# Two of three split score products merged into one 512-column matmul, with two PSUM banks for the scores and two instead of three for the transposes

## The chip, the cores and the metric

One core of one Trainium2 chip runs the program in one launch. The metric is the device time of an execution in microseconds (us), lower is better. The kernel before took 349.04 us as the median of three runs (346.83 to 352.06).

## The reference, cut to what matters

Attention over columns for four batches, whose output feeds a soft mixture of experts. N is 5056 rows, C is 256 columns.

```python
def _attn_ref(q, k, v, tau):                      # (4, 5056, 256) each
    qn = q / (norm(q, axis=1) + 1e-06)
    kn = k / (norm(k, axis=1) + 1e-06)
    s = kn.transpose(0, 2, 1) @ qn / tau          # 256 x 256 per batch, summed over 5056 rows
    a = softmax(s, -1)
    return v @ a

def _moe_ref(x, phi, w1, w2):                     # x: (20224, 256)
    logits = x @ phi                              # 32 slots, 8 experts x 4
    d = softmax(logits, 0)
    slot_out[e] = relu((d.T @ x)[e] @ w1[e]) @ w2[e]
    c = softmax(logits, 1)
    return c @ slot_out
```

## The kernel before, in words

**Tiling.** A batch's 5056 rows come in five chunks of 1024 (the last 960) rows. A chunk of q and k is loaded as two halves, `raw{b}_{ch}_0` and `raw{b}_{ch}_1`, each with four groups `j` of 128 rows; a chunk of v is one tile `v{b}_{ch}`. All loads are issued by SyncE (SP) in program order (L122, L492 to L501): the two halves of a chunk of q and k, then from the eighth chunk on one tile of v behind each. `raw` has five buffers (L129), v has six (VB, L39), and a load waits in SP's queue for its buffer to come free; what stands behind it in the queue waits too.

**Stage A, scores** (`scores_chunk`, L143). Per half, ScalarE rounds the first NS of the four groups to the type fp32r (`hl[:, 0]`, L156), VectorE takes the remainder (`hl[:, 1]`, L157), and ScalarE squares q and k for the norms (L160). TensorE accumulates k^T q over all rows in PSUM tile S, for two halves `m` of k's columns. A split group takes three products with 256 moving columns: high k by high q, high k by low q, low k by high q (L173). An unsplit group takes one product in plain float32, which runs as two matmul instructions. NS is 2 in batch 0 (0 in its first half) and 3 after that. S is one PSUM bank and has one buffer, so batch b+1's first product waits until ScalarE has copied S to `ssb` (L206).

**Attention** (`attention_steps`, L192). The norms go through TensorE (n, nn), then the scale rq, the row maximum, Exp (a), the transpose of a (aTp, L247), and M = a phi (Mp, L254).

**Stage B, soft slots** (`soft_slots`, L469) of batch b runs during stage A of batch b+1, two chunks behind. Each chunk of v is transposed by TensorE in four tiles (vTp, L284) that share the three PSUM buffers of `ps_t` (L64) and are copied out at L291. Then come the logits L (L309), their maximum (peak, rp), the shift (cp, L355), Exp, and `gather_chunk` (G, L397), which multiplies v itself by the weights. G is the last reader of a v tile. Chunks 0 to 2 make the first gather group (G_0) and chunks 3 and 4 the second (G_1).

**Tail and output.** After the last batch's scores, a sequence written out by hand for TensorE (L511 to L692) finishes the last two batches, the experts H and O follow, and then 20 output chunks are computed and stored (L707 to L744).

**What sets the order.** Outside the part by hand, and for SP, a scheduler with its own timeline model decides the order of the instructions on each engine when the program is built, from priorities, buffers and its costs. So an edit in one place can move instructions elsewhere.

Of the kernel before, what the change touches and what calls it, by code (L numbers as in the profile page):

```python
# [8 lines left out]
F32 = mybir.dt.float32  # L9
F32R = mybir.dt.float32r  # L10
AF = mybir.ActivationFunctionType
ALU = mybir.AluOpType
AX = mybir.AxisListType
PSUM = bass.MemoryType.PSUM
# [3 lines left out]
def colnorm_attention_soft_moe(  # L18
# [12 lines left out]
    nc = tc.nc  # L31
    B, N, C = q.shape
    E, _, F = w1.shape
    P = 128
    J = 8
    S = 32
# [16 lines left out]
    while t0 < N:  # L53
        pc = min(P, (N - t0) // J)
# [6 lines left out]
    keep = ctx.enter_context(tc.tile_pool(name="keep", bufs=1))  # L61
    vpool = ctx.enter_context(tc.tile_pool(name="vpool", bufs=VB))
    bpool = ctx.enter_context(tc.tile_pool(name="bpool", bufs=1))
    ps_t = ctx.enter_context(tc.tile_pool(name="ps_t", bufs=3, space=PSUM))  # L64
    ps_b = ctx.enter_context(ExitStack())
    pb = ps_b.enter_context(tc.tile_pool(name="pb", bufs=1, space=PSUM))
    ps_a = ctx.enter_context(ExitStack())
    pa = ps_a.enter_context(tc.tile_pool(name="pa", bufs=1, space=PSUM))
# [54 lines left out]
    st = [dict() for _ in range(B)]  # L123
# [19 lines left out]
    def scores_chunk(b, ch):  # L143
        pc = chunks[ch][1]
        if ch == 0:
            st[b]["S"] = pa.tile([P, 2, C], F32, tag="S", name=f"S{b}")
            st[b]["sum"] = apool.tile([P, G, 2, C], F32, tag="sum", name=f"sum{b}", bufs=1)
        sps, ssum = st[b]["S"], st[b]["sum"]
        sqs = []
        for h in range(2):  # L150
# [12 lines left out]
            for x, j in enumerate(order):  # L163
                first = ch == 0 and h == 0 and x == 0
                last = ch == NCH - 1 and h == 1 and x == HJ - 1
                for m in range(2):
                    cols = slice(P * m, P * m + P)
                    if j >= ns:
                        pairs = [(raw[:pc, 1, j, cols], raw[:pc, 0, j, :])]
                    else:  # L170
                        kh, kl = hl[:pc, 0, 1, j, cols], hl[:pc, 1, 1, j, cols]
                        qh, ql = hl[:pc, 0, 0, j, :], hl[:pc, 1, 0, j, :]
                        pairs = [(kh, qh), (kh, ql), (kl, qh)]  # L173
                    for y, (lhs, rhs) in enumerate(pairs):
                        nc.tensor.matmul(  # L175
                            sps[:, m, :],
                            lhs,
                            rhs,
                            start=first and y == 0 and m == 0,
                            stop=last and y == len(pairs) - 1,  # L180
                            skip_group_check=True,
                        )
        s0, s1 = sqs
# [8 lines left out]
    def attention_steps(b):  # L192
# [4 lines left out]
        for g in range(G):  # L197
# [4 lines left out]
                start=True,  # L202
                stop=True,
            )
        busy = b < B - 1
        nc.scalar.copy(ssb, sps)  # L206
        nc.scalar.copy(nsb, nps)
        yield
        mp = pb.tile([P, 2 * C], F32, tag="amisc", name=f"nn{b}")
# [574 lines left out]
```

## Time and profile before

| | before |
|---|---|
| times of three runs, us | 346.83, 349.04, 352.06 |
| span of the profiled execution, us | 344.0 |
| busy TensorE (PE) / VectorE (DVE) / ScalarE (ACT), us | 304.7 / 250.4 / 237.2 |
| matmuls of the scores, split groups (S<-hl) | 648 instructions, 102.1 us |
| matmuls of the scores, unsplit groups (S<-raw) | 208 instructions, 55.7 us |
| transposes of v (vTp) | 320 instructions, 42.8 us |
| mean granted TensorE clock | 0.972 |

The profile page gives the span from the first to the last instruction of one execution; that execution's own time isn't listed apart, and what lies around the span is about 5 us if it is compared with the median. A row of the timeline view gives start, length, engine, line, operation, tiles and count of a run of equal instructions, and in brackets how long the engine sat idle before it and what ended that. Matmuls are pipelined, so the cost of one is read from start to start and not from its length. PEld is TensorE's weight load, SPq is the queue of SyncE. The stages lie at these times: scores from 7 to 210 us, the tail to about 277 us, the output to 344 us.

### The profile page before, as it was taken

Reading aid. Unit: us, or ns where it says so; the run is one execution under the profiler, and the core shown is the slowest. Engines: PE = TensorE matmul, PEld = TensorE weight load, DVE = VectorE, ACT = ScalarE, POOL = GpSimd, SP = SyncE. Lnnn points to the kernel's source line nnn. Section 1 sums busy time; section 2 is a strip of 40 time slices with the busy share of each in tenths; the row PEclk is TensorE's granted clock in tenths of the full one; section 3 lists DMA queues with packets and bytes.
Section 4 is the critical chain, followed back from the end, with each engine's and each line's share of the span. In section 5 each row is a group of like instructions: output and inputs, shape, how many; then the busy total and the mean of one; then the engine's idle time right before and its main releaser. Section 6 shows DMA issues by size and latency. Waiting matters only on the chain.

```text
span 344.0 us, 6200 instructions
## 1 busy us (share of the span) xinstructions
PE 304.7 (89%) x2460; PEld 238.8 (69%) x2460; DVE 250.4 (73%) x410; ACT 237.2 (69%) x306; POOL 11.4 (3%) x16
## 2 busy tenths in 40 slices
PE   1999969997999999999999899898889998989850
PEld 1888868987788977777896776665644576767530
DVE  1588798995898894988799478478958167986440
ACT  3676769987898995898799396464343348796620
POOL 0000000100000100000100000104000000000000
PEclk9999969999999999899999999999999999999995
DMA  7999989999899429999921994999979408999995
GB/s 248 356 387 243 322 292 326 313 246 356 271 288 340 139 94 265 384 409 266 399 120 29 291 316 104 424 266 412 419 303 418 173 26 342 288 416 356 376 401 209
DMA packets 20244, 100.04 MB, mean 291 GB/s; under 512 B 2744, under 2 KB 2744, under 8 KB 13240
## 3 DMA queue, kind: packets, MB, share of 16 engines
q1 hardware_dynamic: 20216, 99.66, 83.6%
q8 instruction: 19, 0.31, 0.4%
q14 instruction: 9, 0.07, 0.1%
HBM read 78.94 MB, written 20.71 MB: 290 GB/s over the span
## 4 chain that ended last, share of the span: by engine, by line
PE 56%; DMA 15%; DVE 11%; ACT 9%; issue 3%; SPq 2%; POOL 0%; DVEq 0%; ACTq 0%
PE S L175 20%; DMA raw<-in_k_dram 12%; PE vTp L284 7%; PE op L729 5%; PE L L309 4%; PE op L730 4%; DMA v<-in_v_dram 3%; PE G L397 3%; ACT hl L156 3%; ACT sq L160 3%; DVE o L735 2%; PE H L644 2%; PE O L670 2%; PE cTp L718 2%; DVE sq L184 1%
## 5 line engine op out<-in xcount | busy, mean ns | idle before, releaser
L175 PE MATMUL S<-hl 128*128 128x256 f32 (+1 forms) x648 | 102.1, 303 | 2.3 <-DVE hl L157 2.0
L175 PEld LDWEIGHTS S<-hl 128*128 128x128 f32 (+1 forms) x648 | 86.1, 196 | 10.7 <-issue 3.7
L160 ACT ACTIVATE sq<-raw 128x2048 f32<-128x2048 f32 (+1 forms) x40 | 76.8, 1921 | 10.4 <-DMA raw<-in_k_dram 4.7
L157 DVE TENSOR_TENSOR hl<-raw,hl 128x1536 fp32r<-128x1536 f32 (+3 forms) x39 | 63.5, 1628 | 20.8 <-ACT hl L156 20.8
L156 ACT CAST hl<-raw 128x1536 fp32r<-128x1536 f32 (+3 forms) x39 | 53.8, 1379 | 25.4 <-DMA raw<-in_k_dram 13.1
L175 PE MATMUL S<-raw 128*128 128x256 f32 (+1 forms) x208 | 55.7, 401 | 11.7 <-DMA raw<-in_k_dram 9.0
L184 DVE TENSOR_TENSOR sq<-sq,sq 128x2048 f32<-128x2048 f32 (+1 forms) x20 | 45.8, 2288 | 6.9 <-ACT sq L160 6.6
L175 PEld LDWEIGHTS S<-raw 128*128 128x128 f32 (+1 forms) x208 | 38.9, 202 | 16.5 <-issue 9.4
L284 PE MATMUL vTp<-ident,v 128*128 128x128 f32 (+1 forms) x320 | 42.8, 275 | 3.1 <-DMA v<-in_v_dram 2.8
L291 ACT COPY vT<-vTp 128x512 f32<-128x512 f32 (+1 forms) x70 | 39.1, 588 | 8.8 <-PE vTp L284 7.8
L284 PEld LDWEIGHTS vTp<-ident,v 128*128 128x128 f32 (+1 forms) x320 | 35.4, 142 | 9.8 <-issue 6.0
L729 PE MATMUL op<-soh,cT 128*128 128x512 f32 (+1 forms) x80 | 34.1, 426 | 4.5 <-ACT o L733 2.3
L733 ACT COPY o<-op 128x1024 f32<-128x1024 f32 (+1 forms) x26 | 26.3, 1023 | 10.1 <-PE op L730 10.1
L730 PE MATMUL op<-sol,cT 128*128 128x512 f32 (+1 forms) x80 | 31.6, 395 | 0.0
L735 DVE COPY o<-op 128x1024 f32<-128x1024 f32 (+1 forms) x14 | 17.1, 1224 | 13.0 <-PE op L730 13.0
L309 PE MATMUL L<-vT,M 128*32 128x256 f32 (+1 forms) x320 | 22.8, 383 | 1.7 <-DVE cm L566 1.5
L185 DVE TENSOR_TENSOR sq<-sq 128x1024 f32<-128x1024 f32 (+1 forms) x20 | 24.3, 1213 | 0.0
L729 PEld LDWEIGHTS op<-soh,cT 128*128 128x128 f32 (+1 forms) x80 | 14.9, 186 | 12.7 <-DVE o L735 5.7
L397 PE MATMUL G<-v,dn 128*32 128x256 f32 (+1 forms) x320 | 20.0, 382 | 0.5 <-DVE zacc L385 0.5
L723 ACT CAST cT<-cTp 128x512 fp32r<-128x512 f32 (+1 forms) x20 | 11.7, 588 | 10.3 <-PE cTp L718 5.3
L730 PEld LDWEIGHTS op<-sol,cT 128*128 128x128 f32 (+1 forms) x80 | 15.0, 187 | 2.4
L397 PEld LDWEIGHTS G<-v,dn 128*32 128x32 f32 (+1 forms) x320 | 9.8, 109 | 7.0 <-ACT gs L426 1.0
(122 smaller groups left out, 284.6 us busy)
## 6 DMA issues: line engine op xcount, KB each, us to landing
raw<-in_q_dram SPq DMA_DIRECT2D x32, 512.0 KB, 8.2
raw<-in_k_dram SPq DMA_DIRECT2D x32, 512.0 KB, 8.9
v<-in_v_dram SPq DMA_DIRECT2D x16, 1024.0 KB, 9.2
w<-in_moe_w_dram SPq DMA_DIRECT2D x16, 1024.0 KB, 16.5
out_dram<-o SPq DMA_DIRECT2D x15, 1024.0 KB, 6.7
raw<-in_q_dram SPq DMA_DIRECT2D x8, 480.0 KB, 9.6
raw<-in_k_dram SPq DMA_DIRECT2D x8, 480.0 KB, 11.3
v<-in_v_dram SPq DMA_DIRECT2D x4, 960.0 KB, 16.6
```

The costliest lines, as they stand in the source:

```text
L156: nc.scalar.copy(hl[:pc, 0, :, :ns], raw[:pc, :, :ns])
L157: nc.vector.tensor_tensor(hl[:pc, 1, :, :ns], raw[:pc, :, :ns], hl[:pc, 0, :, :ns].bitcast(F32), op=ALU.subtract)
L160: nc.scalar.activation(sq[:pc], raw[:pc], AF.Square)
L175: nc.tensor.matmul(sps[:, m, :], lhs, rhs, start=first and y == 0 and m == 0, stop=last and y == len(pairs) - 1, skip_group_check=True,)
L184: nc.vector.tensor_tensor(s0[:pc], s0[:pc], s1[:pc], op=ALU.add)
L284: nc.tensor.transpose(tp[:, jj, :pc], vt[:pc, 4 * hh + jj, P * m : P * m + P], ident[:pc, :pc])
L291: nc.scalar.copy(dst, tp[:, :, :pc])
L309: nc.tensor.matmul(L[S * g : S * g + S, :, :w], M[:, m, :], st[b]["vT", ch, m][:, :, S * g : S * g + w], start=m == 0, stop=m == 1,)
L397: nc.tensor.matmul(gp[S * g : S * g + S, :], dn[ch - lo][:pc, j, :], vt[:pc, j, :], start=ch == lo and j < G, stop=ch == hi - 1 and j >= G,)
L729: nc.tensor.matmul(dst, cT[:, 2 * hh + jj, :pc], soh, start=True, stop=False)
L730: nc.tensor.matmul(dst, cT[:, 2 * hh + jj, :pc], sol, start=False, stop=True)
L733: nc.scalar.copy(od, op[:pc])
```

## The change

For a split group, high k by high q and high k by low q have the same weights. They become one matmul with 512 moving columns, whose result has two halves: S grows to [128, 2, 2, 256], two PSUM banks, one for each `m`. Low k by high q (256 columns) is added to the second half. The first half holds the high products and the unsplit groups. At the end of a batch ScalarE copies the first half to `ssb`, and VectorE adds the second half to it. To make room, `ps_t` gets two buffers instead of three.

```diff
-    ps_t = ctx.enter_context(tc.tile_pool(name="ps_t", bufs=3, space=PSUM))
+    ps_t = ctx.enter_context(tc.tile_pool(name="ps_t", bufs=2, space=PSUM))
...
-            st[b]["S"] = pa.tile([P, 2, C], F32, tag="S", name=f"S{b}")
+            st[b]["S"] = pa.tile([P, 2, 2, C], F32, tag="S", name=f"S{b}")
...
                     if j >= ns:
-                        pairs = [(raw[:pc, 1, j, cols], raw[:pc, 0, j, :])]
+                        todo = [(sps[:, m, 0], raw[:pc, 1, j, cols], raw[:pc, 0, j, :])]
                     else:
                         kh, kl = hl[:pc, 0, 1, j, cols], hl[:pc, 1, 1, j, cols]
-                        qh, ql = hl[:pc, 0, 0, j, :], hl[:pc, 1, 0, j, :]
-                        pairs = [(kh, qh), (kh, ql), (kl, qh)]
-                    for y, (lhs, rhs) in enumerate(pairs):
+                        todo = [(sps[:, m], kh, hl[:pc, :, 0, j, :]), (sps[:, m, 1], kl, hl[:pc, 0, 0, j, :])]
+                    for y, (dst, lhs, rhs) in enumerate(todo):
                         nc.tensor.matmul(
-                            sps[:, m, :],
+                            dst,
                             lhs,
                             rhs,
-                            start=first and y == 0 and m == 0,
-                            stop=last and y == len(pairs) - 1,
+                            start=first and y == 0,
+                            stop=last and y == len(todo) - 1,
                             skip_group_check=True,
                         )
...
-        nc.scalar.copy(ssb, sps)
+        nc.scalar.copy(ssb, sps[:, :, 0])
+        nc.vector.tensor_tensor(ssb, ssb, sps[:, :, 1], op=ALU.add)
         nc.scalar.copy(nsb, nps)
```

In the changed kernel the lines from the products on stand one higher (the matmul is L174, ScalarE's copy L205), up to the added line, which is L206; behind it the numbers are as before.

The scheduler's order changes with it, above all on TensorE. First place: TensorE in stage A of batch 2, around the gather G_0 of batch 0, which frees the first three v tiles. Before:

```order
118 L175 MATMUL S_1021<-raw_3_0_214 128x256 x2
119 L397 MATMUL G_0_994<-v_0_172,dn_0_991 32x256 x8
120 L397 MATMUL G_0_994<-v_1_180,dn_0_991 32x256 x8
121 L397 MATMUL G_0_994<-v_2_188,dn_0_991 32x256 x8
122 L284 MATMUL vTp_0_1_1_1329<-ident,v_0_212 128x128 x4
123 L175 MATMUL S_1021<-hl_3_0_1350 128x256 x18
124 L175 MATMUL S_1021<-raw_3_1_217 128x256 x2
...
129 L175 MATMUL S_1021<-hl_3_1_1375 128x256 x13
130 L284 MATMUL vTp_1_0_0_1403<-ident,v_1_220 128x128 x4
...
133 L175 MATMUL S_1021<-raw_4_0_222 128x256 x2
```

The same place in the changed kernel, from the last product of hl_3_1 on:

```order
359 L174 MATMUL S_927<-hl_3_1_1239 128x256
...
368 L397 MATMUL G_0_900<-v_0_172,dn_0_897 32x256 x8
369 L397 MATMUL G_0_900<-v_1_180,dn_0_897 32x256 x8
370 L397 MATMUL G_0_900<-v_2_188,dn_0_897 32x256 x4
371 L254 MATMUL Mp_838<-phi_sb,aT_836 128x32 x4
372 L338 MATMUL rp_1_1092<-ident,mx_1_1090 1x128
...
376 L284 MATMUL vTp_1_0_0_1261<-ident,v_1_220 128x128 x4
377 L309 MATMUL L_0_1207<-vT_0_0_1179,M_843 32x256 x4
...
382 L174 MATMUL S_927<-raw_4_0_222 128x256 x2
383 L284 MATMUL vTp_1_1_1_1280<-ident,v_1_220 128x128 x4
384 L309 MATMUL L_1_1286<-vT_1_0_1260,M_843 32x256 x4
385 L174 MATMUL S_927<-hl_4_0_1299 128x512
```

G_0 has moved behind all products of hl_3_0, raw_3_1 and hl_3_1, so that no score product is left between it and raw_4_0; between them now stand the rest of G_0, Mp, rp, five transposed tiles, L_0 and cp.

Second place: TensorE in stage A of batch 3, around G_0 of batch 1. Before:

```order
202 L175 MATMUL S_1630<-hl_3_0_1962 128x256 x4
203 L397 MATMUL G_0_1603<-v_0_212,dn_0_1597 32x256 x8
204 L397 MATMUL G_0_1603<-v_1_220,dn_0_1597 32x256 x8
205 L397 MATMUL G_0_1603<-v_2_228,dn_0_1597 32x256 x8
...
210 L175 MATMUL S_1630<-hl_3_0_1962 128x256 x11
211 L175 MATMUL S_1630<-raw_3_1_258 128x256 x2
212 L175 MATMUL S_1630<-hl_3_1_1987 128x256 x13
213 L338 MATMUL rp_1_1819<-ident,mx_1_1817 1x128
214 L254 MATMUL Mp_1538<-phi_sb,aT_1536 128x32 x4
...
219 L175 MATMUL S_1630<-raw_4_0_263 128x256 x2
220 L175 MATMUL S_1630<-hl_4_0_2053 128x256
```

The same place in the changed kernel:

```order
534 L174 MATMUL S_1477<-hl_3_0_1773 128x256
535 L174 MATMUL S_1477<-raw_3_1_258 128x256 x2
536 L397 MATMUL G_0_1450<-v_0_212,dn_0_1444 32x256 x8
537 L397 MATMUL G_0_1450<-v_1_220,dn_0_1444 32x256 x4
538 L254 MATMUL Mp_1385<-phi_sb,aT_1383 128x32 x4
...
545 L309 MATMUL L_0_1760<-vT_0_0_1732,M_1390 32x256 x4
...
557 L174 MATMUL S_1477<-hl_3_1_1792 128x256
...
562 L174 MATMUL S_1477<-raw_4_0_263 128x256 x2
563 L174 MATMUL S_1477<-hl_4_0_1852 128x512
```

G_0 has moved behind hl_3_0 and raw_3_1; of the products of that chunk only hl_3_1 is left between it and raw_4_0, and the whole of hl_4_0 follows raw_4_0 at once, where one product, L_0 and a tile of vTp stood before.

Third place: VectorE at the end of batch 0, where S is handed over. Before:

```order
29 L187 TENSOR_TENSOR sum_274<-sq_3_0_399 128x512
30 L157 TENSOR_TENSOR hl_0_0_545<-raw_0_0_154,hl_0_0_545 128x1536
31 L184 TENSOR_TENSOR sq_4_0_444<-sq_4_0_444,sq_4_1_465 120x2048
32 L157 TENSOR_TENSOR hl_0_1_570<-raw_0_1_157,hl_0_1_570 128x1536
33 L185 TENSOR_TENSOR sq_4_0_444<-sq_4_0_444 120x2x512
```

In the changed kernel:

```order
29 L186 TENSOR_TENSOR sum_274<-sq_3_0_379 128x512
30 L157 TENSOR_TENSOR hl_0_0_510<-raw_0_0_154,hl_0_0_510 128x1536
31 L183 TENSOR_TENSOR sq_4_0_416<-sq_4_0_416,sq_4_1_433 120x2048
32 L206 TENSOR_TENSOR ssb_454<-ssb_454,S_273 128x512
33 L157 TENSOR_TENSOR hl_0_1_529<-raw_0_1_157,hl_0_1_529 128x1536
```

The new add that releases S stands behind the long addition of the squares sq_4_0. SP's order of loads is the same in both.

## The prediction

> **What bounds the kernel now.** I read the page first, for the share of each engine, then the waits of SP's queue, then TensorE's timeline at the two places where those waits are longest.
>
> ```profile
> PE 304.7 (89%) x2460; PEld 238.8 (69%) x2460; DVE 250.4 (73%) x410; ACT 237.2 (69%) x306; POOL 11.4 (3%) x16
> L175 PE MATMUL S<-hl 128*128 128x256 f32 (+1 forms) x648 | 102.1, 303 | 2.3 <-DVE hl L157 2.0
> L175 PEld LDWEIGHTS S<-hl 128*128 128x128 f32 (+1 forms) x648 | 86.1, 196 | 10.7 <-issue 3.7
> ```
>
> TensorE is busy 89% of a span of 344.0 us, and the products that change are its largest group: 648, so 216 triples. That makes the change look as if it worked on the bound. But a length isn't a cost here, and the second view shows what TensorE is kept waiting for.
>
> ```profile
> SPq L140 <- PE G L397: 34.3, 3, 19.1
> ```
>
> SP stands with a load of v at its head until a gather frees a buffer, 34.3 us in three waits of up to 19.1, and the loads of q and k stand behind it. The two places on SP, and the first on TensorE:
>
> ```profile
> 112.56 0.44 SPq L132 DMA_DIRECT2D raw<-in_k_dram  x1
> 125.35 0.33 SPq L140 DMA_DIRECT2D v<-in_v_dram  x1
> 126.21 0.40 SPq L132 DMA_DIRECT2D raw<-in_k_dram  x1
> 187.02 0.33 SPq L140 DMA_DIRECT2D v<-in_v_dram  x1
> ```
> ```profile
> 124.22 2.80 PE L397 MATMUL G<-v,dn 128*32 128x256 f32 x48
> 126.95 0.66 PE L284 MATMUL vTp<-ident,v 128*128 128x128 f32 x4
> 127.36 2.40 PE L175 MATMUL S<-hl 128*128 128x256 f32 x18
> 129.59 1.03 PE L175 MATMUL S<-raw 128*128 128x256 f32 x4
> 130.27 0.95 PE L175 MATMUL S<-hl 128*128 128x256 f32 x5
> ...
> 135.73 1.10 PE L175 MATMUL S<-raw 120*128 120x256 f32 x4 [0.76 <-DMA raw<-in_k_dram]
> 136.76 0.38 PE L355 MATMUL cp<-negone,rowrun 1*128 1x1 f32 x2
> 137.07 1.08 PE L254 MATMUL Mp<-phi_sb,aT 128*128 128x32 f32 x8
> 137.98 0.36 PE L175 MATMUL S<-hl 120*128 120x256 f32 x1
> 138.99 3.05 PE L175 MATMUL S<-hl 120*128 120x256 f32 x17 [0.64 <-DVE hl L157]
> ```
>
> The reader is to see a race. The first v tile's share of G_0 ends at 124.22 + 2.73/3 = 125.13 us, and 0.2 us later SP issues v and then raw_4_0. That data is usable 10.6 us after the gather (135.73) in raw form and 13.9 us after it (138.99) split. TensorE fills nearly all of this with score products that were loaded earlier, and idles 0.76 + 0.64 = 1.4 us. The same at the second place:
>
> ```profile
> 185.89 2.80 PE L397 MATMUL G<-v,dn 128*32 128x256 f32 x48
> 197.94 1.10 PE L175 MATMUL S<-raw 120*128 120x256 f32 x4 [1.23 <-DMA raw<-in_k_dram]
> 199.43 0.39 PE L175 MATMUL S<-hl 120*128 120x256 f32 x1 [0.39 <-ACT hl L156]
> 201.47 2.29 PE L175 MATMUL S<-hl 120*128 120x256 f32 x17
> ```
>
> So in stage A the time is set by TensorE's work in order plus whatever of this latency it can't fill. Both depend on where the scheduler puts G_0.
>
> **The merged product.** From the chain of waits, the pitch of the 256-column products; from the output stage's timeline, the 512-column products of this type, with a weight load each (the first and the last of four rows in a row).
>
> ```profile
> 80.73 2.05 PE S L175 x17
> ```
> ```profile
> 321.69 0.39 PE L730 MATMUL op<-sol,cT 128*128 128x512 f32 x1
> ...
> 322.38 0.39 PE L729 MATMUL op<-soh,cT 128*128 128x512 f32 x1
> ```
>
> 2.05/17 is 0.121 us; 322.38 - 321.69 is three steps of 0.230 us. A triple goes from 3 x 0.121 = 0.362 to 0.230 + 0.121 = 0.351 us: 11 ns less, times 216 = **2.4 us less**. The streamed columns are the same, and the weight loads already run beside the products (17 of both in 2.05 us). Bounds: the merged product as dear as two gives 0; as cheap as one 256-column product it gives 216 x 0.121 = 26 us. I take 2.4, since the row with the same width is in the trace.
>
> The Trainium skill, "TensorE: Matmul & The Clock Gate", section "Part 3", says that a weight load overlaps matmuls in flight only when the row group differs. By that 216 loads would come off the path; the pitch above speaks against it, and its price stands under the rivals.
>
> **G_0 moved, batch 2.** In the new order (shown above) all score products that can run without the new load stand ahead of G_0. What is left behind G_0's first tile, ahead of raw_4_0, with steps from start to start:
>
> ```profile
> 118.30 1.36 PE L284 MATMUL vTp<-ident,v 128*128 128x128 f32 x11
> 119.41 0.36 PE L175 MATMUL S<-hl 128*128 128x256 f32 x1
> 119.71 1.06 PE L309 MATMUL L<-vT,M 128*32 128x256 f32 x16
> 120.70 2.18 PE L175 MATMUL S<-hl 128*128 128x256 f32 x16
> ```
>
> The rest of G_0, 2 x 0.91; Mp, 137.98 - 137.07 = 0.91; cp, 137.07 - 136.76 = 0.31, and rp priced like it; five tiles of vTp at 4 x 1.11/11 = 0.40, 2.0; L_0, 0.99. Sum 6.3 us. The data comes after 10.6, so TensorE waits 4.3. Then raw_4_0 (130.27 - 129.59 = 0.68), a tile of vTp (0.40) and half of L_1 (0.5) bring it to 12.2, and the first split product, which now reads high and low q at once, waits to 13.9: 1.7 more. Together 6.0 against 1.4: **4.6 us more**. The work that moved ahead isn't lost, it is done in a time that was full anyway; lost is the cover. SP's queue restarts later by the same move, and the transfers keep their length. Bounds: 0, if G_0 comes early enough that TensorE idles ahead of it anyway, to 13.9 - 1.4 = 12.5, if nothing covers it.
>
> **G_0 moved, batch 3.** First tile done at 185.89 + 0.91 = 186.80. Data after 11.1 us (197.94). The split is ready after ScalarE and VectorE, at 197.90 + 1.48 + 1.77 = 201.15, so 14.4 us after the gather:
>
> ```profile
> 137.18 1.77 DVE hl L157
> 197.90 1.48 ACT hl L156
> ```
>
> Left as cover: the rest of G_0 1.8, Mp 0.9, rp and cp 0.6, four tiles of vTp 1.6, L_0 1.0, hl_3_1 6 x 0.351 = 2.1: 8.0 us. Wait 3.1, then raw 0.68, and hl_4_0 waits 14.4 - 11.8 = 2.6. Together 5.7 against 1.23 + 0.39 = 1.6: **4.1 us more**, with bounds as before.
>
> **The clock behind a stall.**
>
> ```profile
> 40.00:50.00 10.00, 7.08 (x34) 6.11 (x33) 9.66 (x8) 8.91 (x7) 0.00 (x0) 0.73 0.91 325
> 140.00:150.00 10.00, 10.00 (x91) 7.75 (x91) 8.39 (x14) 9.19 (x12) 0.00 (x0) 0.83 1.02 413
> 190.00:200.00 10.00, 8.38 (x64) 7.02 (x64) 3.85 (x7) 4.31 (x5) 0.00 (x0) 1.00 1.02 272
> ```
>
> In these windows PEclk (third number from the right) is 0.73 and 0.83 behind idle stretches of TensorE, and 1.00 at the second stall, which was short. 0.83 of 10 us is 3.4 us at half clock, 1.7 us of work. A longer second stall should cost that too: **1.7 us more** (0 to 3.4).
>
> **S is released later.** The end of batch 0:
>
> ```profile
> 45.09 0.56 ACT L206 COPY ssb<-S 128x512 f32<-128x512 f32 x1
> 45.21 2.29 DVE L184 TENSOR_TENSOR sq<-sq,sq 120x2048 f32<-120x2048 f32 x1
> 45.70 2.07 PE L175 MATMUL S<-raw 128*128 128x256 f32 x4 [2.74 <-ACT ssb L206]
> ```
> ```profile
> L187 DVE TENSOR_TENSOR sum<-sq 128x512 f32<-128x512 f32 x16 | 10.8, 678 | 0.1
> ```
>
> The new add stands behind sq_4_0 in VectorE's order, so it starts at 47.5, takes about 0.68 (as the equally wide L187) and lets TensorE on at 48.2 instead of 45.7. That is 2.5 us, of which the clock was half in these windows, so at most 1.3 us of work; as DMA is 0.91 busy there, I count half: **0.7 us** (0 to 2.5). At the end of batch 1 only L_0 (1.0 us) stands between the last product and the next S, against a copy and an add of 0.56 + 0.68 with their handshakes: **0.6 us** (0 to 2). At the end of batch 2 two tiles of vTp, half of L_2 and gtp stand there and cover it.
>
> **Two buffers for the transposes.** In the stalls the waits for them are covered; in the tail, where 8 tiles follow each other at a few places, **0.5 us** (0 to 2). In the output stage the transposes only lose one chunk of lead, 0.
>
> Sum: -2.4 + 4.6 + 4.1 + 1.7 + 0.7 + 0.6 + 0.5 = +9.8 us on a span of 344.0. The span lies 5 us under the median of the runs; what lies around it doesn't change. Forecast 349.0 + 9.8 = **358.8 us**, 2.8% slower.
>
> **The rivals.** First, *the race is relocated but not lost* (not slower): G_0 late in order, but the score products ahead of it find their data late, so that TensorE idles ahead of G_0 and the latency overlaps that idle time. For it: VectorE and ScalarE are near full at 100 to 125 us. Against it: the rows of TensorE shown from 118 to 135 us have no idle time. Then the two stalls and the clock cost nothing net: 349.0 - 2.4 + 1.8 = 348.4 us. It decides from the point where TensorE idles 4 us or more ahead of each G_0.
> Second, *the removed loads were on the path* (faster): 216 x 86.1/648 = 28.7 us less at most; with the stalls still there 349.0 + 9.8 + 2.4 - 28.7 = 332.5 us. Against it stands the pitch of 0.121 us. This is the price from rows of the overlap rule named above, and I give it 0.03.
> Third, *everything adds up*: half clock behind both stalls and the hand-overs at their upper bounds, 358.8 + 1.7 + 1.8 + 1.4 + 1.5 = 365.2 us.
>
> **How the numbers follow.** Forecast 0.54, first rival 0.30, second 0.03, third 0.13. The forecast's own spread is about 4 us; 2% (7 us, about what a measurement of this kernel tells from no change) lies at 356.0. Slower: 0.42 of the forecast and the third, 0.55. Same: 0.12 of the forecast and 0.26 of the first rival, 0.38. Faster: 0.04 of the first rival, which can win when the new order is luckier, and the second, 0.07. The range reaches from the first rival's time to the third's: 348.0 to 365.5 us, with some 0.2 outside.
>
> **What would show it.** Right: products of S with 512 columns at a step of 0.23 us; the row of raw products behind G_0 in batches 2 and 3 with an idle time of 3 to 5 us released by the DMA, and the split ones behind with 1 to 3 us released by VectorE; the first row of S in batch 1 waiting for VectorE's ssb, near 48 us. Wrong: idle rows ahead of G_0, or stalls of under 2 us with TensorE's work ending as early as before; a step near 0.12 us for 512 columns would overturn the first term.

## The result, and the profile after

The changed kernel takes **362.77 us** as the median of four runs (361.09 to 364.42); the kernel before took 348.23 on the same occasion. The ratio is 1.040 with a 95% interval of 1.032 to 1.048: 4% slower, some 14.5 us, where the forecast was 9.8 us. Ratios are taken over undisturbed runs alone and medians over all, so the two can differ a little, and the profiles of e3, e9 and e12 below are of disturbed runs. The profiled execution took 364.42 us with a span of 362.5.

First the page and the waits of SP's queue, in the changed kernel:

```profile
PE 308.0 (85%) x2244; PEld 227.4 (63%) x2244; DVE 253.9 (70%) x414; ACT 237.6 (66%) x306; POOL 14.6 (4%) x16
L174 PE MATMUL S<-hl 128*128 128x256 f32 (+3 forms) x432 | 94.2, 366 | 4.3 <-DVE hl L157 4.1
```
```profile
SPq L140 <- PE G L397: 41.0, 3, 21.1
```

216 matmuls are gone and TensorE is busy 3.3 us longer all the same. Its share fell from 89% to 85% because the span grew by 18.5 us. SP waits 41.0 us for gathers instead of 34.3. Then SP's timeline, and TensorE's at the two places that the prediction speaks of:

```profile
114.97 0.43 SPq L132 DMA_DIRECT2D raw<-in_k_dram  x1
136.56 0.33 SPq L140 DMA_DIRECT2D v<-in_v_dram  x1
...
138.72 0.40 SPq L132 DMA_DIRECT2D raw<-in_k_dram  x1
```
```profile
135.43 2.37 PE L397 MATMUL G<-v,dn 128*32 128x256 f32 x40
...
142.63 0.63 PE L284 MATMUL vTp<-ident,v 128*128 128x128 f32 x4 [2.05 <-DMA v<-in_v_dram]
143.19 1.49 PE L309 MATMUL L<-vT,M 128*32 128x256 f32 x16
144.61 1.97 PE L284 MATMUL vTp<-ident,v 128*128 128x128 f32 x8
...
147.02 1.16 PE L174 MATMUL S<-raw 120*128 120x256 f32 x4
...
150.19 2.04 PE L174 MATMUL S<-hl 120*128 120x512 f32 x10 [1.01 <-DVE hl L157]
...
196.19 1.50 PE L397 MATMUL G<-v,dn 128*32 128x256 f32 x24
...
207.54 1.10 PE L174 MATMUL S<-raw 120*128 120x256 f32 x4 [1.41 <-DMA raw<-in_k_dram]
210.82 2.72 PE L174 MATMUL S<-hl 120*128 120x512 f32 x7 [2.18 <-DVE hl L157]
```

The order is as predicted: G_0 of batch 2's stretch starts at 135.43 (124.22 before), the next load goes out behind it at 136.56, and raw_4_0 runs at 147.02, 11.3 us later than before. The idle time shows in brackets: 2.05 + 1.01 = 3.1 us, and 1.41 + 2.18 = 3.6 us at the second place. Third, the starts of batches 1, 2 and 3 and the wait between the first two; the row behind them is the wait for v in batch 1 of the kernel before:

```profile
46.90 1.65 PE L174 MATMUL S<-raw 128*128 128x256 f32 x3 [4.72 <-DVE ssb L206]
70.98 1.06 PE L284 MATMUL vTp<-ident,v 128*128 128x128 f32 x8 [4.30 <-DMA v<-in_v_dram]
96.47 1.13 PE L174 MATMUL S<-raw 128*128 128x256 f32 x4 [1.91 <-DVE ssb L206]
...
161.94 1.13 PE L174 MATMUL S<-raw 128*128 128x256 f32 x4 [1.05 <-DVE ssb L206]
```
```profile
80.10 0.63 PE L284 MATMUL vTp<-ident,v 128*128 128x128 f32 x4 [2.16 <-DMA v<-in_v_dram]
```

Batch 1 starts 1.2 us later than before (45.70), batch 2 3.7 us later (its first raw product stood at 92.80 before). All three batches now wait for the new add on VectorE; the kernel before waits 2.74 us at the start of batch 1 and has no idle time at the starts of batches 2 and 3. Fourth, stretches of 10 us with the granted clock, the third number from the right:

```profile
40.00:50.00 10.00, 5.28 (x20) 4.21 (x19) 8.95 (x8) 7.20 (x6) 0.00 (x0) 0.74 0.84 308
70.00:80.00 10.00, 9.02 (x47) 7.99 (x48) 4.36 (x6) 4.95 (x6) 0.00 (x0) 0.83 0.81 223
140.00:150.00 10.00, 7.13 (x52) 4.62 (x50) 5.86 (x13) 5.75 (x9) 0.00 (x0) 0.83 1.01 265
210.00:220.00 10.00, 9.18 (x68) 7.01 (x69) 7.37 (x12) 7.16 (x12) 0.00 (x0) 0.73 0.96 284
```

Read in windows of 0.8 us, and as long as TensorE has products left, the clock is at half in stretches of 3.4 us or two of them in a row: before, near 44 and 140 us (10.2 us in all, so 5.1 us lost); after, near 44, 72, 143, 208 and, in the experts' stage, 273 us (23.9 us, 11.9 lost).

**Where the 18.5 us of the two spans lie.** The spans differ by more than the medians do. In every run on record the time is 1.7 to 1.9 us above the span, not the 5 us that a comparison with the median of other executions gave, so the profiled execution of the kernel before took some 345.8 us, less than any of its four timed ones, and that of the changed kernel is its slowest.

Up to the product that ends the experts' stage (fo, 277.6 us before and 291.7 after) it is 14.1 us. Of these, 3.7 come before batch 2 starts and 8.2 from there to the last score product. In that stretch TensorE's idle time, added up from its timeline, grew from 3.0 to 7.7 us (+4.7): 3.6 at the two places behind G_0 and 1.05 at the hand-over of S to batch 3. The time lost at half clock grew from 1.7 to 5.1 us (+3.4), but 1.1 of that falls on the idle time ahead of 210.82 and is counted already, which leaves 2.3. Behind the scores it is 2.2, of which one more stretch at half clock is 1.7. So 3.7 + 4.7 + 2.3 + 1.7 = 12.4 us are placed and 1.7 are not. The other 4.4 us lie behind fo, where the engines do the same work in the same time and only the last transfers land later; whether this part belongs to the change is open, and the last section comes back to it.

### The profile page after: what moved, and what is told of

It is laid out like the page before. It is cut to its first block, busy times and chain, and to the rows that moved or that the text cites. A ratio compares the mean times of both kernels' runs of the same rounds, so it can differ in the third digit from the quotient of the medians.

```text
span 362.5 us, 5767 instructions
## 1 busy us (share of the span) xinstructions
PE 308.0 (85%) x2244; PEld 227.4 (63%) x2244; DVE 253.9 (70%) x414; ACT 237.6 (66%) x306; POOL 14.6 (4%) x16
## 4 chain that ended last, share of the span: by engine, by line
PE 49%; DMA 14%; DVE 14%; ACT 11%; issue 5%; SPq 2%; POOL 1%; DVEq 0%; ACTq 0%; POOLq 0%
PE S L174 18%; DMA raw<-in_k_dram 11%; PE vTp L284 7%; PE op L729 5%; ACT sq L160 5%; PE op L730 4%; DMA v<-in_v_dram 3%; DVE hl L157 3%; PE L L309 3%; PE H L644 2%; PE G L397 2%; PE cTp L718 2%; PE O L670 2%; DVE o L735 2%; DVE sq L184 2%
## 5 line engine op out<-in xcount | busy, mean ns | idle before, releaser
L174 PE MATMUL S<-hl 128*128 128x256 f32 (+3 forms) x432 | 94.2, 366 | 4.3 <-DVE hl L157 4.1
L174 PEld LDWEIGHTS S<-hl 128*128 128x128 f32 (+1 forms) x432 | 71.0, 199 | 20.5 <-DVE hl L157 6.3
L157 DVE TENSOR_TENSOR hl<-raw,hl 128x1536 fp32r<-128x1536 f32 (+3 forms) x39 | 63.5, 1628 | 14.4 <-ACT hl L156 14.1
L174 PE MATMUL S<-raw 128*128 128x256 f32 (+1 forms) x208 | 54.9, 398 | 16.2 <-DMA raw<-in_k_dram 8.5
L174 PEld LDWEIGHTS S<-raw 128*128 128x128 f32 (+1 forms) x208 | 38.5, 200 | 22.7 <-DVE ssb L206 8.6
L284 PE MATMUL vTp<-ident,v 128*128 128x128 f32 (+1 forms) x320 | 45.0, 280 | 8.1 <-DMA v<-in_v_dram 7.0
L284 PEld LDWEIGHTS vTp<-ident,v 128*128 128x128 f32 (+1 forms) x320 | 36.0, 144 | 18.4 <-issue 14.4
L291 ACT COPY vT<-vTp 128x512 f32<-128x512 f32 (+1 forms) x70 | 38.2, 583 | 12.5 <-PE vTp L284 12.4
L309 PE MATMUL L<-vT,M 128*32 128x256 f32 (+1 forms) x320 | 24.4, 390 | 1.5 <-DVE cm L566 1.5
L735 DVE COPY o<-op 128x1024 f32<-128x1024 f32 (+1 forms) x14 | 17.1, 1225 | 11.9 <-PE op L730 11.9
L729 PEld LDWEIGHTS op<-soh,cT 128*128 128x128 f32 (+1 forms) x80 | 14.9, 186 | 11.9 <-ACT o L733 4.9
L214 POOL TENSOR_TENSOR rn<-rn,half 128x4 f32<-128x4 f32 x4 | 7.9, 1970 | 166.9 <-DVE rn L213 116.5
## 6 DMA issues: line engine op xcount, KB each, us to landing
w<-in_moe_w_dram SPq DMA_DIRECT2D x16, 1024.0 KB, 15.1
```

What stands on the lines that cost most here:

```text
L157: nc.vector.tensor_tensor(hl[:pc, 1, :, :ns], raw[:pc, :, :ns], hl[:pc, 0, :, :ns].bitcast(F32), op=ALU.subtract)
L174: nc.tensor.matmul(dst, lhs, rhs, start=first and y == 0, stop=last and y == len(todo) - 1, skip_group_check=True,)
L284: nc.tensor.transpose(tp[:, jj, :pc], vt[:pc, 4 * hh + jj, P * m : P * m + P], ident[:pc, :pc])
L291: nc.scalar.copy(dst, tp[:, :, :pc])
L309: nc.tensor.matmul(L[S * g : S * g + S, :, :w], M[:, m, :], st[b]["vT", ch, m][:, :, S * g : S * g + w], start=m == 0, stop=m == 1,)
L729: nc.tensor.matmul(dst, cT[:, 2 * hh + jj, :pc], soh, start=True, stop=False)
```

## The experiments

The theory was the prediction's: the order that came with the merged product puts G_0 late, the next load of q and k queues behind it, and TensorE runs dry. The rivals: the merged product itself, the two banks with their add, or something else in the new order. All the runs beside each other first; "idle" and "lost" are TensorE's idle time, and the time lost to half clock, from the first product of batch 2 to the last of batch 3 in the profiled execution; half clock that falls on idle time is in both. The ratio is to the kernel before, timed on the same chip.

| kernel | median us | ratio, 95% interval | batch 2 starts | batch 3 ends | idle | lost |
|---|---|---|---|---|---|---|
| before | 348.2 | 1 | 92.8 | 209.7 | 3.0 | 1.7 |
| changed | 362.77 | 1.040 [1.032, 1.048] | 96.5 | 221.6 | 7.7 | 5.1 |
| e1 changed, scores behind G_0 | 363.24 | 1.040 [1.031, 1.048] | 93.1 | 217.9 | 8.8 | 3.4 |
| e2 before, G_0 late | 359.53 | 1.031 [1.022, 1.040] | 94.8 | 223.0 | 8.3 | 1.7 |
| e3 unmerged | 349.60 | 0.997 [0.992, 1.003] | 97.4 | 208.2 | 0.0 | 0 |
| e10 unmerged, again | 350.51 | 1.010 [1.007, 1.014] | 94.7 | 206.1 | 0.5 | 0 |
| e4 merged, order of e3 | 350.25 | 1.006 [1.000, 1.013] | 95.4 | 205.4 | 0.0 | 0 |
| e11 the same, again | 354.93 | 1.018 [1.011, 1.025] | 98.4 | 212.6 | 1.5 | 3.1 |
| e5 unmerged, changed order | 363.14 | 1.035 [1.023, 1.046] | 95.7 | 221.0 | 6.8 | 5.1 |
| e6 changed, 7 v buffers | 358.98 | 1.029 [1.021, 1.037] | 98.2 | 215.8 | 3.5 | 3.4 |
| e7 before, 7 v buffers | 344.36 | 0.989 [0.983, 0.995] | 93.0 | 206.5 | 0.0 | 0 |
| e8 changed order, 7 v buffers | 354.15 | 1.022 [1.018, 1.027] | 96.8 | 213.9 | 3.2 | 0 |
| e9 order of e3, 7 v buffers | 351.45 | 0.999 [0.992, 1.006] | 100.5 | 211.7 | 0.0 | 1.7 |
| e12 as e8, add earlier | 351.80 | 1.018 [1.010, 1.026] | 96.8 | 213.9 | 3.2 | 0 |

**e1: undo the place of G_0 in the changed kernel.** The split products of chunk 3 in batches 2 and 3 are queued behind G_0.

```diff
+                        g0 = st[b - 2].get("G0") if b >= 2 and ch == 3 and j < ns else None
+                        with tc.issue_after(g0) if g0 is not None else nullcontext():
-                        nc.tensor.matmul(
+                            nc.tensor.matmul(
...
-            nc.tensor.matmul(
+            t = nc.tensor.matmul(
...
+        if gi == 0 and ch == hi - 1:
+            st[b]["G0"] = t.ins
```

> The changed kernel, complete, with one constraint on the order: the split products of chunk 3 of batches 2 and 3 stand behind the gather G_0 of the batch before last, as they roughly did before the change. Theory (the new order places G_0 late, SP's queue restarts late, and the latency of its loads lies bare): the idle time of TensorE at raw_4_0 and hl_4_0 falls from 3.1 and 3.6 us to under 2 us each, and the time falls by 7 to 11 us from 362.8 to 352 to 356 us. Rival A (the later release of S and the two transpose buffers cost by themselves, wherever G_0 stands): 360 us or more. Rival B (the merged product is itself dearer): 360 us or more.

Measured: 363.24 us, nothing won, so by its time e1 fits the two rivals and not the theory. TensorE's timeline of this kernel, where line 176 is the score product and 399 the gather:

```profile
126.78 0.66 PE L286 MATMUL vTp<-ident,v 128*128 128x128 f32 x4 [1.67 <-ACT vT L293]
...
129.87 2.37 PE L399 MATMUL G<-v,dn 128*32 128x256 f32 x40 [0.41 <-DVE sm L242]
...
142.38 1.03 PE L176 MATMUL S<-raw 120*128 120x256 f32 x4
145.25 1.07 PE L176 MATMUL S<-hl 120*128 120x512 f32 x4 [1.85 <-DVE hl L157]
```

and VectorE's row for the weights `dn` that G_0 multiplies by, in this kernel, in the changed one and in the one before:

```profile
128.86 0.95 DVE L370 STREAM_TRANSPOSE dn<-lt 128x768 f32<-128x768 f32 x1
```
```profile
132.28 0.95 DVE L368 STREAM_TRANSPOSE dn<-lt 128x768 f32<-128x768 f32 x1
```
```profile
119.52 0.97 DVE L368 STREAM_TRANSPOSE dn<-lt 128x768 f32<-128x768 f32 x1
```

The reader is to see that G_0 starts as soon as `dn` is done (128.86 + 0.95 = 129.81), with TensorE idle ahead of it; the bracket names the short instruction behind `dn` on the same engine. It couldn't have come earlier. Not G_0 alone but the whole chain that feeds it, from the logits through the maximum and the shift, stands later in the new order: `dn` by 12.8 us in the changed kernel and by 9.3 us here. Even in the changed kernel `dn` is done only 2.2 us before G_0 starts (132.28 + 0.95 against 135.43). The score products that were held back lost as cover what they gave as lead: idle 8.8 us instead of 7.7. The waits at raw_4_0 and hl_4_0 did shrink, to 1.85 us and, at the second place, 2.18; the others grew. So the theory needed an amendment: the order decides, but G_0's place is the last link of it, and moving that link by itself buys nothing.

**e2: the reverse, a late G_0 in the kernel before.** The gathers of batches 0 and 1 are queued behind the chunk-3 products of batches 2 and 3.

```diff
-                        nc.tensor.matmul(
+                        st[b]["mm"] = nc.tensor.matmul(
...
-                gather(b, gi)
+                (late.append((b, gi)) if b < 2 else gather(b, gi))
...
+            if ch == NCH - 2 and b >= 2:
+                with tc.issue_after(st[b]["mm"].ins):
+                    for ch2 in range(*groups[b - 2][0]):
+                        gather_chunk(b - 2, 0, ch2)
+                finish(b - 2, 0)
+                gather(b - 2, 1)
```

> The kernel before, complete, with nothing of the change in it but the place of the gathers: those of batches 0 and 1 stand behind the last split product of chunk 3 of batches 2 and 3. Theory: TensorE idles 3 to 6 us at each of the two places, waiting for raw_4_0 and hl_4_0, and the time rises by 7 to 11 us to 355 to 360 us. Rivals A and B: it stays within 3 us of the kernel before, at 346 to 351 us.

Measured: 359.53 us, in the theory's range. Three of TensorE's rows with idle time behind the two late gathers:

```profile
139.86 2.82 PE L284 MATMUL vTp<-ident,v 128*128 128x128 f32 x12 [2.06 <-DMA v<-in_v_dram]
...
147.69 1.57 PE L175 MATMUL S<-hl 120*128 120x256 f32 x11 [0.36 <-DVE hl L157]
...
211.34 1.10 PE L175 MATMUL S<-raw 120*128 120x256 f32 x4 [1.09 <-DMA raw<-in_k_dram]
```

Late gathers make the old kernel 3% slower, with the same releasers as in the changed kernel. Behind the first gather TensorE idles 2.4 us, less than the 3 to 6 expected, and behind the second 3.2. The scheduler also moved other work of TensorE along with the gathers, so e2 isn't as clean as the square below. Idle time and half clock grew by 5.3 us together and batch 2 started 2.0 us later; the rest of some 10 us isn't placed.

**e3: one part alone.** The changed kernel with its two banks, add and two vT buffers, but with three products of 256 columns.

```diff
-                        todo = [(sps[:, m], kh, hl[:pc, :, 0, j, :]), (sps[:, m, 1], kl, hl[:pc, 0, 0, j, :])]
+                        qh, ql = hl[:pc, 0, 0, j, :], hl[:pc, 1, 0, j, :]
+                        todo = [(sps[:, m, 0], kh, qh), (sps[:, m, 1], kh, ql), (sps[:, m, 1], kl, qh)]
```

> The changed kernel with the merged product taken apart again: three products of 256 columns into the two banks; the two banks, the add on VectorE and the two transpose buffers stay. The scheduler then places G_0 ahead of the products of hl_3_0 in batch 2 and ahead of raw_3_0 in batch 3, so early or earlier than before the change. Theory: no stall over 2 us at raw_4_0, and 350 to 355 us, what the hand-overs and buffers cost and no more. Rival A: 358 us or more, since all that it blames is still there. Rival B: about 348 us.

Measured: 349.60 us, level with the kernel before (350.51 and 1% above it when repeated, as e10). That lies between the theory's 350 to 355 and rival B's 348. The banks, the add and the buffers aren't the loss, or at most 1% of it. But this edit also gives another order, so it doesn't yet tell the merged product from the order.

**e4 and e5: the square.** To part the two, the order itself is written down. A table in the kernel names, for TensorE, ScalarE and VectorE, the place of every instruction, and an edge without a wait ties each to the one ahead of it. SP's order is the program's in all these kernels. e4 has merged products in the order of e3; e5 has three products in the order of the changed kernel.

```diff
+    pin(tc, nc)
+
+PIN = {
+    "PE": [
+        "0-115 133-153 116-119 154-163 120-123 217-224 164-177 225-232 178-191 124 269-276 192-205 277-284",
...
+def pin(tc, nc):
...
+        for x, y in zip(place, place[1:]):
+            tc.add_manual_dep(
+                mine[y],
+                mine[x].name,
+                mybir.DependencyInfo(mybir.DependencyClass.NoSync, mybir.DependencyReason.DATA),
+                reason="order",
+            )
```

> The changed kernel, its merged products kept, but the instructions of TensorE, ScalarE and VectorE are forced into the order that the kernel with three 256-column products (previous experiment, 349.6 us) has. Theory (the loss sits in the order that came with the merged product, not in the product): 346 to 350 us, G_0 of batch 2 near 125 us, and the merged product worth 0 to 2.4 us beside 349.6. Rival (the merged product itself costs, since its first product waits for high and low q of the whole half): 355 us or more.

> The other corner of the same square: three 256-column products, two banks, the add, but TensorE, ScalarE and VectorE forced into the order of the changed kernel (each merged product replaced by its two at the same place). Theory (order alone): 361 to 367 us, as the changed kernel or up to 2.4 us above it, with raw_4_0 of batch 2 near 147 us. Rival (the merged product itself): 349 to 353 us.

Measured: e4 350.25 us, e5 363.14 us. Whichever product is used, the changed kernel's order costs some 13 us by the medians (363.14 - 350.51 with e10 below, 362.77 - 350.25; with e11 below in e4's place it is 7.8). These kernels ran on several chips; by the ratios to the kernel before on the same chip it is 2.2 to 3.4%, some 8 to 12 us. Whichever order is used, the merged product changes nothing that these times show. TensorE's timeline of e4 at the first place, and its SP wait:

```profile
122.95 2.35 PE L397 MATMUL G<-v,dn 128*32 128x256 f32 x34
...
139.39 0.60 PE L174 MATMUL S<-raw 120*128 120x256 f32 x2
...
140.58 1.62 PE L174 MATMUL S<-hl 120*128 120x512 f32 x7
```
```profile
SPq L140 <- PE G L397: 38.1, 3, 17.2
```

G_0 is at 122.95, and no row up to raw_4_0 and the split products behind it has a bracket. SP still waits 38.1 us, more than in the kernel before (34.3), and TensorE doesn't idle for it here, for it has other work. In e5 the brackets are back, at or close to the places where the changed kernel has them:

```profile
145.62 1.88 PE L175 MATMUL S<-raw 120*128 120x256 f32 x4 [1.45 <-DMA raw<-in_k_dram]
...
207.69 2.04 PE L175 MATMUL S<-raw 120*128 120x256 f32 x4 [2.54 <-DMA raw<-in_k_dram]
210.97 1.44 PE L175 MATMUL S<-hl 120*128 120x256 f32 x5 [1.02 <-DVE hl L157]
```

The difference closes within 1 us. From batch 2's start to batch 3's end the changed kernel takes 125.1 us and e4, with the same products, 110.0: 15.1 more. Of that 7.7 is idle time and 5.1 half clock, with 1.1 counted in both. The remaining 3.4 is in the main work that the changed kernel does here and e4 behind the scores, where e4 takes 2.6 us longer (54.0 against 51.4 us from the last score product to the first of the experts).

**e6 and e7: take away what makes the load wait.** A seventh buffer for v, in the changed kernel and, as a control, in the one before. The room comes from the first expert's weights, which are now loaded with the others.

```diff
-    VB = 6
+    VB = 7
...
-    w1t[0] = keep.tile([P, 2, F], F32, name="w1_0")
...
-        if i == WI:
-            nc.sync.dma_start(w1t[0], w1[0].rearrange("(p d) f -> p d f", d=2))
...
-        for e in range(max(1, G * r), G * r + G):
+        for e in range(G * r, G * r + G):
```

> The changed kernel with seven buffers for v instead of six (the room comes from w1 of the first expert, which is loaded with the other weights, later). The load of raw_4_0 no longer queues behind a load of v that waits for G_0. Theory of the prediction (the stalls behind G_0 are the loss): idle time of TensorE at raw_4_0 and hl_4_0 of batches 2 and 3 falls from 6.7 us to under 2, the half clock behind it goes too, 353 to 357 us. Rival (the whole work of the earlier batch runs late, and G_0 is only its last visible part): 360 us or more.

> The kernel before with the same seventh buffer, as a control. Its stalls behind G_0 were 3.0 us together, so at most that is to be had: 345 to 350 us by either theory. If it is over 352 us, the later load of the first expert's weights has a price of its own, which then has to be taken off the run with seven buffers in the changed kernel.

Measured: 358.98 and 344.36 us. Both gained some 4 us, so the distance stayed, which fits neither expectation for e6 well. Its trace says why. The scheduler gave a new order again, with raw_4_0 ahead of G_0, so the stall at raw_4_0 is gone, and another idle stretch came up further on:

```profile
137.77 0.62 PE L397 MATMUL G<-v,dn 128*32 128x256 f32 x2
...
155.93 1.08 PE L309 MATMUL L<-vT,M 128*32 128x256 f32 x8 [3.53 <-DVE nat L327]
```

As an experiment on the buffer e6 is spoiled: it moves two things. In the kernel before, where the order changed as well, the seventh buffer leaves no idle time in batches 2 and 3 (3.0 us without it) and no half clock there; e7 is the fastest kernel of this study, 1.1% below the kernel before (0.5 to 1.7%).

**e8: the seventh buffer, with the changed kernel's order held fast** by the same kind of table.

> The changed kernel with seven buffers for v, but this time TensorE, ScalarE and VectorE are forced into exactly the order of the changed kernel, so that the buffer is the only difference (in the run before the scheduler had also given another order). Theory of the prediction (the load of raw_4_0 waits for G_0 through the v buffer): TensorE's idle time at raw_4_0 and hl_4_0 of batches 2 and 3 falls to under 2 us, the batches take 4 to 8 us less together, 354 to 358 us. Rival (the whole work of the earlier batch stands late in the order, and another load waits instead): 360 us or more.

Measured: 354.15 us, inside the theory's range. The four places in its timeline, and its SP wait:

```profile
144.05 1.13 PE L174 MATMUL S<-raw 120*128 120x256 f32 x4
...
147.21 2.38 PE L174 MATMUL S<-hl 120*128 120x512 f32 x12 [1.03 <-DVE hl L157]
...
203.09 1.13 PE L174 MATMUL S<-raw 120*128 120x256 f32 x4
...
205.12 2.27 PE L174 MATMUL S<-hl 120*128 120x512 f32 x11 [0.90 <-DVE hl L157]
```
```profile
SPq L140 <- PE G L397: 28.2, 3, 14.8
```

Of the 6.7 us at these places 1.9 are left, both waits for a transfer are gone, and so is the half clock in batches 2 and 3. From batch 2's start to batch 3's end it takes 117.1 us instead of 125.1. The idle time fell by 4.5 and the half clock by 5.1; that is more than the 8.0 us, since 1.1 us of the half clock fell on idle time and is counted in both. By the medians it is 8.6 us, by the ratios 1.8% or some 6. So the load that waits for the gather, in this order, is 6 to 8.6 of the 14.5 us lost, about half, unless part of the gain comes with a seventh buffer in any order, which e9 leaves open. For the other half no experiment names a single cause.

**e9: the buffer in the good order.** The table of e4 with seven buffers.

> Merged products, seven buffers for v, and the order of the kernel with three 256-column products. With six buffers this order left TensorE no idle time in batches 2 and 3, so by the theory (a buffer helps only where a load waits behind a late gather) the seventh gains under 1.5 us: 348 to 351 us beside about 350. Rival (the buffer is worth its 4 us in any order, as it was in the kernel before and in the changed one): 344 to 347 us, level with the kernel before with seven buffers (344.4).

Measured: a median of 351.45 us over twelve runs from 343.45 to 354.68, with a ratio of 0.999 [0.992, 1.006] beside e4's 1.006 [1.000, 1.013]. The intervals overlap: the times exclude neither the theory's gain of under 1.5 us nor the rival's 4. The traces agree with the theory, as neither kernel has idle time in batches 2 and 3 for the buffer to take away.

**e10 and e11: e3 and e4 again, side by side, to size the product.**

> Three 256-column products with two banks, the add and two vT buffers again, as the partner of the next run on the same chip. By the first measurement 348 to 351 us, within 1% of the kernel before.

> Merged products in the order of the run before, on the same chip, to size the product by itself: the order of every engine is the same, so the difference of the two medians is the price of the merge. The prediction's term: 2.4 us less than the run before. Rival (a first product that waits for high and low part of q, or the same pitch per column, eats it): within 1 us of it or above.

Measured: 350.51 and 354.93 us; the ratios are 1.010 [1.007, 1.014] and 1.018 [1.011, 1.025]. The merged product isn't 2.4 us faster; whether it is slower is open, since the same kernel gave 1.006 in e4. In the trace its gain is there and small. One half of a chunk has six triples. In the prediction's rows of the kernel before, 18 products of hl start at 127.36 and the raw products behind them at 129.59: 2.23 us. In the changed kernel, 12 products:

```profile
112.15 2.37 PE L174 MATMUL S<-hl 128*128 128x512 f32 x12
114.36 1.03 PE L174 MATMUL S<-raw 128*128 128x256 f32 x4
```

2.21 us. Over 36 such halves 0.02 us is 0.7. From the start of batch 3 to the end of its fourth chunk, 48 triples in one order without idle time, e3 and e10 take 45.06 us and e4 and e11 44.73; times 216/48 that is 1.5. Both lie under the scatter from run to run.

**e12: the hand-over of S.** As e8, but at the ends of batches 0 and 1 the add stands one place earlier on VectorE. The edit swaps two pairs of neighbours in the table, of which the first is shown (39 is the add, 35 the squares):

```diff
-        "0-15 18 16-17 19-20 23 21-22 24-25 28 26 29 27 33 30 34 31-32 52 35 39 53 36-38 54 57 55-56 58 40 59",
+        "0-15 18 16-17 19-20 23 21-22 24-25 28 26 29 27 33 30 34 31-32 52 39 35 53 36-38 54 57 55-56 58 40 59",
```

> As the run with seven buffers in the changed kernel's own order (354.15 us), with one edit: at the ends of batches 0 and 1 the add that finishes ssb stands one place earlier in VectorE's order, ahead of the squares it stood behind. The first raw product of batch 1 should start near 44.8 us instead of 46.5, that of batch 2 by 1 to 3 us earlier than 96.8. The prediction counted half of the 2.5 us of the first hand-over as lost: by that the time falls by 0.7 to 1.3 us, to 352.8 to 353.5. Rival one (the later batch starts of the changed kernel, 3.8 us at batch 2, come from this add altogether): 350 to 351 us. Rival two (the transfers set the pace of batch 1 and nothing is gained): 354 us, batch 2 at 96 to 97 us as before.

Measured: 351.80 us against 354.15, with ratios of 1.018 and 1.022 whose intervals overlap. TensorE's waits in the profiled execution, which took 356.6 us:

```profile
45.41 2.08 PE L174 MATMUL S<-raw 128*128 128x256 f32 x4 [3.09 <-DVE ssb L206]
58.23 1.06 PE L284 MATMUL vTp<-ident,v 128*128 128x128 f32 x8 [1.96 <-DMA v<-in_v_dram]
72.12 1.09 PE L284 MATMUL vTp<-ident,v 128*128 128x128 f32 x4 [5.17 <-DMA v<-in_v_dram]
96.84 1.13 PE L174 MATMUL S<-raw 128*128 128x256 f32 x4 [1.33 <-DVE ssb L206]
```

The add came earlier and batch 1 starts 1.1 us earlier (46.5 in e8), but the waits for v in the middle of the batch grew (from 0.23 and 4.18 us in e8 to 1.96 and 5.17), and batch 2 starts at 96.8 in both. So in this trace the transfers set the pace of batch 1, and the place of the add is worth nothing by batch 2 (rival two). The times alone would allow the theory, and rival one too, so e12 doesn't decide.

## Why the prediction came out as it did

The time was forecast at 358.8 us in a range of 348.0 to 365.5 and measured at 362.8: the side held, and of the mechanism that the order and the loads behind the gather cost the time; three sizes didn't, and G_0's own place was not the lever.

**What held.** The cause: the new order, not the product, the banks or the add. The square of e3, e4, e5 and the changed kernel shows it, and e8 shows that the load behind the gather is about half of it. The prediction took G_0's place in the queue for the cause of its lateness; e1 shows that its inputs come late as well, so that moving G_0 alone wins nothing. The latencies too: G_0's first tile ends at 135.43 + 0.92 = 136.35, and the first split product runs at 150.19, 13.8 us later (13.9 forecast); at the second place the raw products come 10.4 and the split ones 13.7 us after it (11.1 and 14.4). At the second place both waits have the releasers that were named, at the first only the split product's has: no row of raw products shows the 3 to 5 us that were to be seen, but 0 and 1.41.

**The stalls, 4.6 + 4.1 us, came out at 3.6 together, and the clock, 1.7 us, at 3.4, or 2.3 outside idle time.** The forecast had 6.0 and 5.7 us of idle time where there were 3.1 and 3.6. The step that failed is not the list of what is left as cover behind G_0: the rows above show the very pieces that the forecast named, five tiles of vTp (four instructions each) and one L ahead of raw_4_0, another tile and half an L behind it. It is their length. From the end of G_0's first tile to raw_4_0 TensorE has 147.02 - 136.35 - 2.05 = 8.6 us of work where the forecast counted 6.3, above all because the clock was at half from 143 to 147 us; at the second place it is 9.0 instead of 8.0. The end of the stretch is set by the data, so a slower cover doesn't make it longer, it only turns idle time into half clock. To add 1.7 us of clock to idle times worked out at full clock was to count some of it twice, and the measured sum, 3.6 + 2.3 = 5.9 us, is below the 10.4 forecast. The wait also fell elsewhere, on a transpose of the next v (2.05 us) ahead of raw_4_0, because that tile comes by the same late queue.

**The hand-over of S, 0.7 + 0.6 us, and the two vT buffers, 0.5, came out at 3.7 us at the start of batch 2, and 1.05 more at batch 3.** Batch 1 starts 1.2 us late, near the forecast. Batch 2 waits 1.91 us for the add where 0.6 were counted, and batch 3 waits 1.05 us, though the forecast held that end to be covered by two tiles of vTp, half of L_2 and gtp. Inside batch 1 the wait for v is 4.30 us instead of 2.16, and half clock costs 1.1 us more than before. Which part of the change this comes from is open. With two banks, batch 2 starts between 93.1 and 98.4 us in eight profiled executions (all but e3, e9 and e12), the same instructions in the same order at 95.4 and at 98.4 (e4, e11); with one bank it started at 92.8, 93.0 and 94.8. The trace of e12 speaks against the place of the add, its times don't decide. A kernel with two vT buffers and one bank in an otherwise unchanged order wasn't tried. In e3 the whole package costs between nothing and 1%, since the stalls of the kernel before go at the same time.

**Luck.** The time came out within 4.0 us of the forecast, but stalls that were counted too large made up for losses that the sum had small or at nothing: the starts of batches 2 and 3, half clock in the experts' stage (1.7 us) and, in these two executions, the last transfers (4.4 us).

**The merged product, -2.4 us, came out at -0.7 to -1.5 in the traces** and can't be seen in the times. The step from the output stage's products of this width was right within 3%: a merged product takes 0.236 us from start to start (0.230 forecast).
The Trainium skill, "TensorE: Matmul & The Clock Gate", section "Part 3", says that a weight load overlaps matmuls in flight only when the row group differs, and so would promise more: here 216 loads went and six triples take 2.21 us instead of 2.23. The trace doesn't agree with that rule, and the second rival is out.

**The rivals.** That the race is only relocated needed 4 us of idle time ahead of each G_0: in the changed kernel there is none from 98 to 140 us, nor from 163 to 206. It does describe e1, where TensorE idles 0.41 us ahead of G_0 and 1.67 us a little earlier. The sum of all upper bounds, 365.2 us, lies 2.4 us above the measured time, the forecast 4.0 below it: by the number the third rival is the nearer. Half clock came out at its upper bound (3.4 us) and the start of batch 2 near that of the hand-overs, but the stalls well below the forecast, so not everything added up.

## What to carry to other kernels

Where a scheduler orders the work, an edit has two prices, the instructions and the order that they bring, and a table that pins the order of every engine tells them apart with two kernels; each is to be timed more than once, for e4 and e11 are one kernel and their medians, from two chips, lie 4.7 us apart. A long wait in a load queue (38.1 us in e4) need not cost anything as long as the engine that sets the time has other work ready; look at what that engine does meanwhile. And the last link of a late chain isn't worth moving before the trace shows when its inputs are ready.

## What the runs showed of the hardware that was not expected

**The last transfers.** From fo on, the engines' work takes the same time in all kernels (the last copy of the output ends 55.9 to 56.5 us behind the start of fo), but the execution ends 65.7 to 71.4 us behind it. e4 and e10 have the same order there; the row of fo and the span of each:

```profile
277.73 0.70 PE L691 MATMUL fo<-ob,fold 128*128 128x256 f32 x2
```
```profile
core 0: 344.4 us, clock 0.975
```
```profile
278.58 0.70 PE L692 MATMUL fo<-ob,fold 128*128 128x256 f32 x2
```
```profile
core 0: 349.1 us, clock 0.966
```

344.4 - 277.7 = 66.7 us, and 349.1 - 278.6 = 70.5. Before and after have 66.4 and 70.8. This isn't plain scatter between executions: e11, which is e4 again, has 65.7, and e3, the kernel of e10, has 71.1. It isn't the slow order either, for e5 has 70.3 with that order and e10 70.5 without it. What makes the transfers slow in some kernels stays open. Up to fo alone e5 takes 12.4 us more than e10 (291.0 against 278.6), so the price of the order doesn't rest on this part.

**The clock.** Half clock came in stretches of 3.4 us, or two in a row, also behind short waits: 1.85 us in e1 (145.25), which its window shows, but not behind 1.03 us in e8 (147.21), nor behind 1.91 us in the changed kernel (96.47), so the runs give no length of wait that decides it.

```profile
140.00:150.00 10.00, 8.15 (x38) 6.21 (x35) 4.67 (x7) 7.34 (x7) 0.00 (x0) 0.83 1.02 329
```
```profile
140.00:150.00 10.00, 8.73 (x69) 6.43 (x68) 7.04 (x15) 8.96 (x14) 0.00 (x0) 1.00 0.95 329
```

The Trainium skill, "TensorE: Matmul & The Clock Gate", section "Part 1", "What's actually happening", gives a free-running window of 3413 ns, and the length of the stretches agrees. The same page of the Trainium skill warns in its section "HAM oscillation" of gaps over about 3.4 us; here gaps of about half that were followed by half clock in some places, so the measurement is the stricter of the two.
